# Dense query and output layouts in a fused state-space and attention kernel: both transposed between partitions through DRAM

## The chip, the cores and the metric

The kernel runs on one core of a Trainium2 chip. The metric is the device time of one execution in microseconds (us), and the kernel before is given by the median of three runs. The engines are TensorE (PE; its weight loads are listed as PEld), VectorE (DVE), ScalarE (ACT), GpSimd (POOL) and SyncE (SP), which here issues nearly all DMAs.

## The reference

Two independent parts share a sequence of 2048 rows and a width of 640, and their outputs are put side by side.

```python
# A: complex diagonal state-space layer
h = Lam_bar[None, :] * h + Bu[:, t, :]          # for t in range(2048)
y = 2.0 * einsum("blp,dp->bld", hseq, Cmat).real + x * Dskip
# B: attention, 32 query heads of width 20, one key head and one value head
q = (x @ wq).reshape(B, S, 32, 20).transpose(0, 2, 1, 3)
k = x @ wk ; v = x @ wv                          # [1, 2048, 20]
p = softmax(einsum("bhqd,bkd->bhqk", q, k) * 20 ** -0.5)
o = einsum("bhqk,bkd->bhqd", p, v)
b = o.transpose(0, 2, 1, 3).reshape(B, S, 640) @ wo
```

## The kernel before, in words

**Units.** The queries are cut into 4 blocks of 512 rows (`NQB`), the 32 heads into 8 groups of four (`NGG`), so that there are 32 groups in order. In a group, head j of the four lies on partitions 32j to 32j+31: 20 rows of the head, then one row (row 20), then unused rows. A unit is one head against 128 keys: 4 x 16 = 64 units for each group and 2048 in all. For each unit PE computes 128x512 scores into PSUM, an engine turns them into exponentials in SBUF, and PE multiplies these by the values into the PSUM tile `PV`, whose row 20 of each head collects the softmax denominator.

**Two engines make exponentials.** ACT takes tiles of three and two units (`R`, L1122, `ex_op`) and writes `P`. DVE takes single units (L1127, `dx_op`), which lie in one of the two PSUM banks `B`: it makes a 16-bit integer whose bits are an approximate exponential, and three shifted copies of it (L1132, `sh_op`, up to three units at once, in `Pd`). At most 16 of a group's 64 units may go to DVE (`QUOTA`).

**Who decides.** `main()` is a planner which runs while the program is built. It keeps a modelled clock for each engine, takes the candidate that could begin first (with biases and a little noise drawn from `SEEDS`, one seed for each 64th of the units), and appends it to that engine's list. Each engine then executes its list in order. A unit goes to DVE when DVE's modelled backlog is short and one of the two `B` banks is free. The same two banks serve the query projections, the output projections and all of part A, so each of these holds a bank from its first matmul to its DVE eviction. Threads of background work (`qt`, `norm`, `proj`, and the threads of part A) wait on gates and are mixed in.

**Queries before.** `qt_block` computes one group with `wq4`, the weights padded to 32 columns for each head: five matmuls of 512 columns, one for each 128 of the width; an absolute value on DVE (L702, into `Qabs`); a sixth matmul with `Mblk`, which adds to row 20 a bound of the scores, so that the exponent can't overflow; and a scaling eviction on DVE (L706) into `QT`, a ring of six groups. Group 0 has ACT take the absolute value. The padded weights are copied by DVE (L550) from `wq_raw`, which lies in the tile `OT`.

**Outputs before.** When a group is finished, DVE copies `PV` to `OTr` (L1165). `norm_ops` then sends the four denominator rows to DRAM and reads them back as 128x16, DVE inverts them (L872), and the inverses go to DRAM and come back spread over 32 partitions each (`rwide`, four DMAs). POOL multiplies into `OT` in four pieces of 128 columns (L885). After the eighth group `proj_ops` multiplies `OT` by the padded `WO4`: for each of 4 row tiles and 2 halves of the columns eight matmuls of 320 columns, and a DVE eviction (L936). The last group's denominators are inverted through PE instead (`norm_last`), and `last_ops` does the last block's rest on PSUM that has come free.

**Start and end.** SP issues the transposed loads of x, then `wq`, then ten transposes of part A's input (blocks 0 and 1, `load_xa`), then ten of `BTre` and `BTim`, then `WO4` and ten transposes of C. The first ACT tile starts when keys and the first queries are there.

Of the kernel before, what the change touches and what calls it, by code (L numbers as in the profile page):

```python
# [9 lines left out]
ALU = mybir.AluOpType  # L10
AX = mybir.AxisListType
FP32 = mybir.dt.float32
# [231 lines left out]
class _Kernel:  # L244
# [4 lines left out]
    TILES, PTILES, DUNITS, DSHIFT, QRING = (3, 2), 10, 9, 3, 6  # L249
# [15 lines left out]
    SEEDS = (0, 102003, 103002, 104005, 0, 0, 107005, 0, 109003, 110001, 111003, 112005, 0, 0, 115003, 116004,  # L265
             117001, 118008, 119004, 120009, 121009, 122003, 123005, 124007, 125004, 126001, 127008, 128001,
             129006, 130003, 131008, 132001, 133004, 134007, 135004, 136007, 137001, 138005, 0, 140005, 141001,
             142007, 143003, 144003, 145008, 146005, 147007, 148002, 149003, 150004, 0, 152009, 0, 154009,
             155008, 156002, 157003, 158008, 159005, 160002, 0, 162006, 0, 164007)
# [24 lines left out]
    def alloc(self):  # L294
# [3 lines left out]
                  for i, n in enumerate(self.TILES)]  # L298
# [9 lines left out]
        self.sb("wq4", [128, NC, self.NGG, 128], BF16)  # L308
        self.sb("Mblk", [128, 128], BF16)
        self.sb("mabs", [128, 5], FP32)  # L310
        self.sb("Qabs", [128, 512], I32)

        self.Qpos = self.Qabs[:].bitcast(BF16).rearrange("p (n h) -> p n h", h=2)[:, :, 1]
        self.sb("WO4", [128, self.NGG, 640], BF16)
# [13 lines left out]
        self.sb("OT", [128, self.NGG, 512], BF16)  # L328
        self.wq_raw = self.OT[:].rearrange("p g n -> p (g n)")[:, 0:NC * 640].rearrange("p (c n) -> p c n", c=NC)
        self.part = self.wq4[:].rearrange("p c g n -> p (c g n)").bitcast(FP32)[:, 0:1280].rearrange("p (t n) -> p t n", t=2)  # L330
        self.sb("rden", [128, 2, 16], BF16)
        self.sb("rwide", [128, 512], BF16)
        self.den_rows, self.rec_rows = (nc.dram_tensor(n, (2, 4, 512), BF16, kind="Internal").ap()
                                        for n in ("den_rows", "rec_rows"))
# [29 lines left out]
        self.sb("ystage", [128, 640], BF16)  # L364

# [52 lines left out]
    def setup(self):  # L418
# [44 lines left out]
        dve(lambda e: e.memset(K.wq4[:], 0.0), writes=["wq4"], n=5120, rate=4)  # L463
# [7 lines left out]
        for j in range(4):  # L471
            act(lambda e, j=j: e.activation(K.wk4[:, :, 32 * j:32 * j + 20], K.wk_raw[:, :, :], ACT.Copy),
                ["wk_raw", "wk4"], ["wk4"], n=100)
        ot = [k for g in range(8) for k in self.ot_keys(g)]
        go(self.dma(K.wq_raw, t["wq"].rearrange("(c p) n -> p c n", p=128), "wq", writes=["wq_raw"] + ot, kb=800))
        wq4_0 = K.wq4[:, :, 0, :].rearrange("p c (j r) -> p c j r", r=32)[:, :, :, 0:20]
        self.tables(dve, act, {
            2: lambda: dve(lambda e: e.tensor_copy(wq4_0, K.wq0.rearrange("p c (j r) -> p c j r", r=20)),
                           ["ostage0", "wq4"], ["wq4_0"], n=400, rate=3.5)})
# [44 lines left out]
        for o in copy("act", 0):  # L524
# [14 lines left out]
        wq4_ap = bass.AP(tensor=K.wq4, offset=128, ap=[[NC * self.NGG * 128, 128], [1024, NC], [32, 28], [1, 20]])  # L539
        wqr_ap = bass.AP(tensor=K.OT, offset=80, ap=[[self.NGG * 512, 128], [640, NC], [20, 28], [1, 20]])  # L540
# [9 lines left out]
            Op("dve", lambda e: e.tensor_copy(wq4_ap, wqr_ap), ["wq_raw", "wq4"] + ot, ["wq4_4"], occ=dve_t(2800, 3.5))])  # L550
# [5 lines left out]
        for b in range(2):  # L556
            for o in self.load_xa(b):
                go(o)
        for c in range(NC):
            go(self.dma(K.BTre[:, c, :], t["bre"][:, 128 * c:128 * (c + 1)], f"bre{c}", writes=[f"BTre{c}"],  # L560
                        tr=True, kb=160))
            go(self.dma(K.BTim[:, c, :], t["bim"][:, 128 * c:128 * (c + 1)], f"bim{c}", writes=[f"BTim{c}"],
                        tr=True, kb=160))

# [123 lines left out]
    def qt_block(self, qb, gg, hold=None, gate=None, done=None):  # L688
# [7 lines left out]
        def mm(c):  # L696
            return self.mms([self.m1(lambda: h.T[:, :], K.wq4[:, c, gg, :], K.xbT[:, c, 512 * qb:512 * qb + 512],
                                     c == 0, False)], ["wq4_0" if gg == 0 else "wq4_4"] + xs, [None], accum=c > 0,
                            lock=c == 0, gate=gate if c == 0 else None, hold=h)
# [3 lines left out]
                                                      op0=ALU.bitwise_and), [None], ["Qpos"], occ=dve_t(512), hold=h),  # L703
# [4 lines left out]
        ]  # L708


    def scan_ops(self):
# [5 lines left out]
        self.prog = prog = dict(x=1, a=0, u=0, s=0, r=0, y=0, w=0, c=0)  # L717
# [13 lines left out]
        for gg in range(self.NGG):  # L731
            pool(lambda e, gg=gg: e.memset(K.WO4[:, gg, :], 0.0), [], ["WO4"] + old, 240)
        wov = t["wo"].rearrange("(gg jr) n -> jr gg n", jr=80)
        for j in range(4):
            sc_.append(self.dma(K.WO4[32 * j:32 * j + 20, :, :], wov[20 * j:20 * j + 20, :, :], f"wo{j}", reads=["WO4"],
                                writes=[f"WO4_{j}"], kb=200))
# [32 lines left out]
        sx = [o for b in (2, 3) for o in self.load_xa(b, lambda b=b: prog["y"] >= 4 * (b - 1), lambda b=b: prog.update(x=b))]  # L769
# [87 lines left out]
    def ot_keys(self, gg):  # L857

        return [f"OT{gg}{h}" for h in self.PIECES]

    def norm_ops(self, g):

        K, sl, gg = self, g % 2, g % self.NGG
        if g == self.NQB * self.NGG - 1:
            return self.norm_last(g)
        den, rec = self.den_rows[sl], self.rec_rows[sl]
        rows = bass.AP(tensor=K.OTr, offset=2 * 512 * self.DH + 512 * sl, ap=[[32 * 2 * 512, 4], [1, 512]])
        flat = lambda x: x.rearrange("j (b n) -> (j b) n", n=16)

        def recip(e):  # L870
            with self.nc.allow_low_precision("bf16 reciprocal of softmax denominator"):
                return e.reciprocal(K.rden[:, sl, :], K.rden[:, sl, :])  # L872
        ops = [self.dma(den, rows, f"den{sl}", reads=[f"OTr{sl}"], writes=[f"den{sl}"], kb=4),
               self.dma(K.rden[:, sl, :], flat(den), f"dens{sl}", reads=[f"den{sl}"], writes=[f"rden{sl}"], kb=4),
               Op("dve", recip, [f"rden{sl}"], [f"rden{sl}"], occ=0.17),
               self.dma(flat(rec), K.rden[:, sl, :], f"rec{sl}", reads=[f"rden{sl}"], writes=[f"rec{sl}"], kb=4)]
        for j in range(4):
            wide = bass.AP(tensor=rec.tensor, offset=rec.offset + 512 * j, ap=[[0, 32], [1, 512]])
            ops.append(self.dma(K.rwide[32 * j:32 * j + 32, :], wide, "rwide", reads=[f"rec{sl}"], writes=[f"rwide{j}"],
                                kb=32))  # L880
        n = 512 // len(self.PIECES)
        gate = lambda: g < self.NGG or g // self.NGG - 1 in self.projected
        for i, h in enumerate(self.PIECES):
            c = slice(n * i, n * i + n)
            ops.append(Op("pool", lambda e, c=c: e.tensor_tensor(K.OT[:, gg, c], K.OTr[:, sl, c], K.rwide[:, c], ALU.mult),  # L885
                          [f"OTr{sl}", *(f"rwide{j}" for j in range(4))], [f"OT{gg}{h}"], occ=max(0.2, n / 450.0 + 0.1),
                          gate=None if i else gate))
        ops[-1].done = lambda: self.normed.add(g)
        return ops

    def norm_last(self, g):
        K = self
        sl, rs, gg = g % 2, g % 2, g % self.NGG
# [8 lines left out]
        def wide(t, j):  # L902
# [5 lines left out]
        ops.append(Op("dve", lambda e: e.tensor_tensor(K.OT[:, gg, :], K.OTr[:, sl, :], h1.T[:, :], ALU.mult),  # L908
                      [None, f"OTr{sl}"], self.ot_keys(gg), occ=dve_t(512), free=True, hold=h1,
# [3 lines left out]
    def proj_ops(self, qb, ggs, part=False):  # L913

        K = self
        ops = []
        wo = ["WO4"] + [f"WO4_{j}" for j in range(4)]
        ots = [k for gg in ggs for k in self.ot_keys(gg)]
        for ts in ((2, 3) if part else range(4)):
            st = ts % 2  # L920
            t0 = 512 * qb + 128 * ts
            for h in range(2):
                hd = Hold()
                lst = [self.m1(lambda hd=hd: hd.T[:, 0:320], K.OT[:, gg, 128 * ts:128 * ts + 128],
                               K.WO4[:, gg, 320 * h:320 * h + 320], gg == ggs[0], gg == ggs[-1]) for gg in ggs]
                have = lambda: all(self.NGG * qb + gg in self.normed for gg in ggs) and (
                    not part or len(self.qt_done) == self.NQB * self.NGG)
# [6 lines left out]
                if part:  # L934
                    dst, keys = K.part[:, st, 320 * h:320 * h + 320], [f"part{st}", "wq4_0", "wq4_4"]
# [7 lines left out]
    def last_ops(self, gates, normed):  # L943

        K = self
        wo = ["WO4"] + [f"WO4_{j}" for j in range(4)]
# [4 lines left out]
        def mm(ts, gg, begin):  # L951
            return self.mms([self.m1(banks[ts][h], K.OT[:, gg, 128 * ts:128 * ts + 128],
                                     K.WO4[:, gg, 320 * h:320 * h + 320], begin, gg == self.NGG - 1) for h in range(2)],
                            self.ot_keys(gg) + wo, keys[ts], accum=not begin, gate=lambda: gates[ts]() and normed(gg))

        threads = []
        for ts in (3, 0, 2, 1):
            t0 = 512 * (self.NQB - 1) + 128 * ts
            first = 0 if ts < 2 else self.NGG - 2
# [426 lines left out]
```

## Time and profile before

| what | value |
|---|---|
| median of 3 runs | 780.4 us (780.14 to 781.43) |
| profiled execution, own time | 780.05 us |
| its span, first to last instruction | 778.3 us |
| granted TensorE clock, mean | 0.993 |
| busy: PE, DVE, ACT, POOL | 698.2, 711.2, 763.1, 450.9 us |
| first ACT tile starts, last one ends | 21.95 us, 768.56 us |
| units through ACT, through DVE | 1647, 401 |
| moved by DMA | 21.08 MB, mean 27 GB/s |

The span is what the profile covers; the own time of the execution is 1.75 us longer. "Busy" is the time in which an engine executes at least one instruction. In the groups of instructions, the columns are line, engine, operation, output and input with their shapes, count, then busy time and mean duration of one in ns, and last the idle time of the engine just before them with what ended it. Durations of neighbours on one engine can overlap by some tens of ns. The unit counts are those of the PV matmuls that read `P` (1647), and of L1127 (401).

### The profile page before, as it was taken

The numbers are of one execution on the slowest core, as the hardware profiler recorded it, in microseconds if no ns is written. First come the engines' busy times: TensorE is split into PE (matmuls) and PEld (weight loads), VectorE is DVE, ScalarE is ACT, GpSimd is POOL, SyncE is SP. The second block draws the span as 40 slices with busy tenths as digits, with TensorE's granted clock in tenths as the row PEclk, the third lists the DMA queues.
The fourth block names the chain that finished last, engine by engine and source line by source line (L and its number), as shares of the span: only waits on it lengthen the run. The fifth ranks groups of instructions, "written<-read, shape, count | busy, mean of one in ns | idle before, by whom it ended". The sixth has DMA issues, their size and how long they took to land.

```text
span 778.3 us, 16683 instructions
## 1 busy us (share of the span) xinstructions
PE 698.2 (90%) x6474; PEld 219.3 (28%) x6538; DVE 711.2 (91%) x1270; ACT 763.1 (98%) x692; POOL 450.9 (58%) x897
## 2 busy tenths in 40 slices
PE   5898887888889999988889999998899999899887
PEld 1322222222223332322223323222233332233223
DVE  7789999999999888899999888999998899998995
ACT  7999999999999999999999999999999999999995
POOL 4418836998995030398895005999960799910010
PEclk9799999999999999999999999999999999999999
DMA  9781000000000000110000001100000000000001
GB/s 191 120 137 27 8 2 8 15 3 9 8 9 18 18 25 17 46 22 9 1 9 17 25 19 39 40 5 9 9 17 25 11 26 10 24 17 25 11 12 38
DMA packets 57877, 21.08 MB, mean 27 GB/s; under 512 B 48332, under 2 KB 57800, under 8 KB 57800
## 3 DMA queue, kind: packets, MB, share of 16 engines
q1 hardware_dynamic: 55658, 19.70, 11.8%
q8 instruction: 52, 0.85, 0.5%
q10 hardware_dynamic: 2142, 0.32, 0.3%
q14 instruction: 25, 0.20, 0.1%
HBM read 5.99 MB, written 5.50 MB: 15 GB/s over the span
## 4 chain that ended last, share of the span: by engine, by line
ACT 86%; DVE 6%; PE 5%; SPq 1%; DMA 1%; issue 1%; DVEq 0%
ACT P L1122 86%; PE R L409 2%; DVE Pd L1132 2%; DVE Pd L1127 2%; PE PV L409 1%; SPq L390 1%; PE B L409 1%; DVE tm L790 1%; DMA xbT<-in_B_x_dram 1%; DVE hh L817 0%; DVE mabs L518 0%; DVE CGre L749 0%; DVE ostage L936 0%; DVE QT L706 0%; DVE CGim L749 0%
## 5 line engine op out<-in xcount | busy, mean ns | idle before, releaser
L1122 ACT ACTIVATE P<-R 128x1536 bf16<-128x1536 f32 (+1 forms) x659 | 745.5, 1443 | 1.5 <-PE B L409 0.7
L409 PE MATMUL R<-QT,KT 32*128 32x512 bf16 (+1 forms) x1647 | 258.6, 387 | 55.5 <-ACT P L1122 45.7
L1127 DVE TENSOR_SCALAR Pd<-B 128x512 int16<-128x512 f32 x401 | 272.1, 683 | 36.4 <-PE B L409 32.1
L1132 DVE TENSOR_SCALAR Pd<-Pd 128x1536 int16<-128x1536 int16 (+2 forms) x534 | 256.9, 514 | 1.0
L409 PE MATMUL PV<-P,VP 128*32 128x512 bf16 x1647 | 246.2, 387 | 1.2 <-issue 0.5
L409 PE MATMUL PV<-Pd,VP 128*32 128x512 bf16 x1604 | 244.9, 384 | 2.4 <-DVE OTr L1165 1.4
L806 POOL TENSOR_TENSOR tm<-hh,cs 128x128 bf16<-128x128 f32 x320 | 161.5, 525 | 12.8 <-DVE hh L817 3.3
L409 PE MATMUL B<-QT,KT 32*128 32x512 bf16 x401 | 154.2, 384 | 0.0
L409 PEld LDWEIGHTS R<-QT,KT 32*128 32x128 bf16 (+1 forms) x1647 | 63.5, 91 | 294.6 <-ACT P L1122 285.6
L885 POOL TENSOR_TENSOR OT<-OTr,rwide 128x128 bf16<-128x128 bf16 x124 | 60.4, 506 | 137.7 <-DMA rwide<-rec_rows 72.5
L806 POOL TENSOR_TENSOR uh<-tm 128x128 bf16<-128x128 bf16 x160 | 80.3, 520 | 72.1 <-DVE tm L790 67.6
L806 POOL TENSOR_TENSOR W<-tm 128x128 bf16<-128x128 bf16 x160 | 90.8, 589 | 13.8 <-PE B L409 9.5
L409 PEld LDWEIGHTS PV<-Pd,VP 128*32 128x32 bf16 x1604 | 58.4, 94 | 62.5 <-issue 39.3
L409 PEld LDWEIGHTS PV<-P,VP 128*32 128x32 bf16 x1647 | 57.7, 94 | 60.5 <-issue 46.7
L747 POOL TENSOR_SCALAR tm<-W,sc 128x128 f32<-128x128 bf16 x40 | 30.8, 783 | 37.0 <-DMA W<-in_A_C_im_dram 19.4
L790 DVE TENSOR_TENSOR tm<-B,cs 128x1024 bf16<-128x1024 f32 x40 | 48.5, 1213 | 2.2 <-PE B L409 2.1
L409 PE MATMUL B<-CGre,W 128*128 128x384 bf16 (+1 forms) x160 | 46.4, 305 | 0.0
L409 PE MATMUL B<-CGim,W 128*128 128x384 bf16 (+1 forms) x160 | 45.5, 299 | 0.0
L409 PE MATMUL B<-xbT,wq 128*128 128x512 bf16 x141 | 41.9, 384 | 3.4 <-issue 1.9
L409 PE MATMUL B<-WO,OT 128*128 128x320 bf16 x220 | 41.0, 302 | 0.0
L817 DVE TENSOR_TENSOR_SCAN hh<-sc,hini,uh 128x512 f32<-128x512 f32 x30 | 40.9, 1365 | 0.0
L409 PEld LDWEIGHTS B<-QT,KT 32*128 32x128 bf16 x401 | 36.3, 90 | 0.0
(130 smaller groups left out, 411.8 us busy)
## 6 DMA issues: line engine op xcount, KB each, us to landing
rwide<-rec_rows SPq DMA_DIRECT2D x124, 32.0 KB, 1.9
out_dram<-ystage SPq DMA_DIRECT2D x16, 160.0 KB, 1.8
out_dram<-ostage SPq DMA_DIRECT2D x12, 160.0 KB, 1.8
OT<-in_B_wq_dram SPq DMA_DIRECT2D x1, 800.0 KB, 6.3
WO<-in_B_wo_dram SPq DMA_DIRECT2D x4, 200.0 KB
den_rows<-OTr SPq DMA_DIRECT2D x31, 4.0 KB
rden<-den_rows SPq DMA_DIRECT2D x31, 4.0 KB, 1.7
rec_rows<-rden SPq DMA_DIRECT2D x31, 4.0 KB, 1.4
```

Of the source, the lines that this page charges most:

```text
L390: return e.dma_start_transpose(out_ap, in_ap)
L409: ins = e.matmul(o() if callable(o) else o, lhsT=l, rhs=r, start=st, stop=sp, skip_group_check=True, **kw)
L747: pool(lambda e, y=y, c=c, gy=gy, i=i: e.tensor_scalar(K.ctmp[:, i:i + 128], y[:, i:i + 128], sc[:, gy, c:c + 1], None, op0=ALU.mult), key ...
L790: dve(lambda e, k=k, h=h: e.tensor_tensor(K.tm[:, 2 * k:2 * k + 2, :], bass.AP(tensor=K.BB, offset=512 * int(h.key[1]), ap=[[512 * self.BA ...
L806: put(lambda e, c0=c0, end=end: e.tensor_tensor(out[:, c0:end], a[:, c0:end], b[:, c0:end], op), reads, [writes + h], n, gate=None if i el ...
L817: dve(lambda e, ri=ri, ini=ini: e.tensor_tensor_scan(K.hh[:, ri, :], dec, K.uh[:, ri, :], ini, ALU.mult, ALU.add), ["sc", *(f"uh{ri}{h}" f ...
L885: ops.append(Op("pool", lambda e, c=c: e.tensor_tensor(K.OT[:, gg, c], K.OTr[:, sl, c], K.rwide[:, c], ALU.mult), [f"OTr{sl}", *(f"rwide{j ...
L1122: return Op("act", lambda e: e.activation(dst, K.R[n % 2][:, 0:512 * size], ACT.Exp, scale=self.exp_scale), [f"R{n % 2}"] + ["R0c"] * (siz ...
L1127: return Op("dve", lambda e: e.tensor_scalar(K.Pd[:, 0, u, :], K.B[x][:, :], self.d_off, 0.0, op0=ALU.add, op1=ALU.max), [f"B{x}"], [f"Pd{ ...
L1132: return Op("dve", lambda e: e.tensor_scalar(K.Pd[:, i, a:b, :], K.Pd[:, 0, a:b, :], float(self.SHIFTS[i]), 0.0, op0=ALU.subtract, op1=ALU ...
```

## The change

The queries of a block are computed without padding and brought to the padded layout by a trip through DRAM; the outputs go through DRAM in the other direction and are projected in a dense layout.

- **Queries.** Groups 0 and 1 keep the old path (weights `wq0p` and `wq1`). For the rest `qd_block` computes a whole block: `wqd` holds the weights with heads innermost, made by five copies on POOL, and five dense tiles of 128 rows take five matmuls and one DVE eviction each into `Qd`. The bound for all 32 heads takes five 16-bit absolute values on DVE and five matmuls with `Md`, and one DVE eviction (`Gs`). Four DMAs write `Qd` and one writes `Gs` to DRAM (`Qs`), and `qr_ops` reads one group at a time into `QT`, now a ring of four. The next block's rows are written when all groups of the block before have been read.
- **Outputs.** A group's `OTr` goes to DRAM whole (`Os`). After the eighth group `dense_ops` reads the denominators (`rwide`, four DMAs) and the outputs (`OTd`, four DMAs) of the block densely, DVE inverts 128x512 at once, and POOL multiplies 5 x 4 pieces. `proj_ops` then takes five matmuls where it took eight. In the last block the groups 6 and 7 take the path of `norm_last` into `OTp`; five dense parts and two padded ones make the sum.
- **Setup.** `wq_raw` lies in the ACT tiles `P7` to `P9` instead of `OT`; new memsets, masks and small DMAs make `Md` and the constant rows in DRAM (`dense_setup`). Part A's input of block 1 is loaded by the planner's thread `sx` and no longer ahead of `BTre`. `WO4` takes eight DMAs instead of four.
- **Planner.** The thread `qt` joins those that can keep units from DVE when they wait for a bank (`starved`); SP's issues for these trips go first; `SEEDS` are others.

```diff
-    TILES, PTILES, DUNITS, DSHIFT, QRING = (3, 2), 10, 9, 3, 6
+    TILES, PTILES, DUNITS, DSHIFT, QRING = (3, 2), 10, 9, 3, 4
...
-        self.wq_raw = self.OT[:]...
+        self.wq_raw = self.P[:].rearrange("p s n -> p (s n)")[:, 18 * 512:18 * 512 + NC * 640].rearrange("p (c n) -> p c n", c=NC)
...
-            Op("dve", lambda e: e.tensor_copy(wq4_ap, wqr_ap), ["wq_raw", "wq4"] + ot, ["wq4_4"], occ=dve_t(2800, 3.5))])
+            Op("dve", lambda e: e.tensor_copy(pad(K.wq1[:]), K.wq_raw[:, :, 80:160].rearrange("p c (j r) -> p c j r", r=20)),
+               ["wq_raw", "wq1"] + pk, ["wq1"], occ=dve_t(400, 3.5))])
+        for c in range(NC):
+            pool(lambda e, c=c: e.tensor_copy(K.wqd[:, c, :].rearrange("p (d h) -> p d h", h=32),
+                                              K.wq_raw[:, c, :].rearrange("p (h d) -> p d h", d=20)),
+                 ["wq_raw"] + pk, [f"wqd{c}"], occ=1.6)
+        self.dense_setup(pool)
-        for b in range(2):
-            for o in self.load_xa(b):
-                go(o)
+        for o in self.load_xa(0):
+            go(o)
...
+    def qd_block(self, qb):
+        gate = lambda: self.units >= 64 * (self.NGG * (qb - 1) + 1)
+        for m in range(NC):
+            h = Hold()
+            for c in range(NC):
+                ops.append(self.mms([self.m1(lambda h=h: h.T[:, :], K.wqd[:, c, 128 * m:128 * m + 128],
+                                             K.xbT[:, c, 512 * qb:512 * qb + 512], c == 0, c == NC - 1)],
...
+            ops.append(Op("dve", lambda e, m=m, h=h: e.tensor_scalar(K.Qd[:, m, :], h.T[:, :], self.c1, None, op0=ALU.mult),
+                          [None], [f"Qd{m}"], occ=dve_t(512), free=True, hold=h))
+        read = lambda: self.qread >= self.NGG * qb
...
+        seq = ["a", "a", "g", "a", "g", "a", "g", "a", "g", "g"]
...
+    def qr_ops(self, g, done):
+        return [self.dma(K.QT[:, r, :], K.Qs[0, 128 * (g % self.NGG):128 * (g % self.NGG) + 128, :], f"QT{r}",
...
+                         gate=lambda: g // self.NGG in self.qsent and self.units >= 64 * (g - self.QRING + 2))]
...
     def norm_ops(self, g):
-        ops = [self.dma(den, rows, ...), self.dma(K.rden[:, sl, :], flat(den), ...),
-               Op("dve", recip, [f"rden{sl}"], [f"rden{sl}"], occ=0.17),
-               self.dma(flat(rec), K.rden[:, sl, :], ...)]
+        return [self.dma(self.Os[qb, 128 * gg:128 * gg + 128, :], self.OTr[:, g % 2, :], f"Os{g % 2}", reads=[f"OTr{g % 2}"],
+                         writes=[f"Os{qb}_{gg}"], kb=128, done=lambda: self.normed.add(g))]
+    def dense_ops(self, qb):
+        for dd in range(4):
+            ops.append(self.dma(K.rwide[32 * dd:32 * dd + 32, :], src, "rwide", ...))
+        for dd in range(4):
+            ops.append(self.dma(K.OTd[32 * dd:32 * dd + 32, :, :], src, "OTd", ...))
+                return e.reciprocal(K.rwide[:], K.rwide[:])
+        ops.append(Op("dve", recip, rw, rw, occ=dve_t(512)))
+        for i, h in enumerate(self.PIECES):
+            for m in range(NC):
+                ops.append(Op("pool", lambda e, c=c, m=m: e.tensor_tensor(K.OTd[:, m, c], K.OTd[:, m, c], K.rwide[:, c], ALU.mult),
...
-                lst = [self.m1(..., K.OT[:, gg, 128 * ts:128 * ts + 128], K.WO4[:, gg, 320 * h:320 * h + 320], ...) for gg in ggs]
+                lst = [self.m1(lambda hd=hd: hd.T[:, 0:320], K.OTd[:, m, 128 * ts:128 * ts + 128],
+                               K.WO4[:, m, 320 * h:320 * h + 320], m == 0, m == NC - 1) for m in range(NC)]
...
         self.starved = dict(sy=r.choice((0.0, 1.0, 4.0, 99.0)), sa=r.choice((2.0, 99.0)),
-                            proj=r.choice((0.0, 1.0, 4.0, 99.0)))
+                            proj=r.choice((0.0, 1.0, 4.0, 99.0)),
+                            qt=r.choice((0.0, 1.0, 4.0, 99.0)))
...
+                if o.eng == "sp" and name in ("qt", "qr", "norm", "dense"):
+                    bias = -2.0
+                elif name == "qt" and not self.qsent:
+                    bias -= 0.1
```

`dve_t(n, rate)` is the planner's price of a DVE instruction, n / (960 x rate) + 0.07 us.

## The prediction

> **What bounds the kernel now.** I read the page from the top: busy shares, slices, chain of waits, then the groups of instructions.
>
> ```profile
> span 778.3 us, 16683 instructions
> PE 698.2 (90%) x6474; PEld 219.3 (28%) x6538; DVE 711.2 (91%) x1270; ACT 763.1 (98%) x692; POOL 450.9 (58%) x897
> DVE  7789999999999888899999888999998899998995
> ACT  7999999999999999999999999999999999999995
> ...
> ACT 86%; DVE 6%; PE 5%; SPq 1%; DMA 1%; issue 1%; DVEq 0%
> ...
> L1122 ACT ACTIVATE P<-R 128x1536 bf16<-128x1536 f32 (+1 forms) x659 | 745.5, 1443 | 1.5 <-PE B L409 0.7
> L1127 DVE TENSOR_SCALAR Pd<-B 128x512 int16<-128x512 f32 x401 | 272.1, 683 | 36.4 <-PE B L409 32.1
> L1132 DVE TENSOR_SCALAR Pd<-Pd 128x1536 int16<-128x1536 int16 (+2 forms) x534 | 256.9, 514 | 1.0
> ```
>
> ACT makes exponentials from 21.95 to 768.56 us, 746.6 us, and in these it idles for about 1. So the span is 22 us of start, the ACT tiles, and 9.7 us of tail, and the middle is shortened only by giving units to DVE. One unit costs ACT 745.5/1647 = 0.453 us, and DVE (272.1 + 256.9)/401 = 1.32 us. DVE is full early and has room later, as the view by stages (PE, PEld, DVE, ACT, POOL) shows:
>
> ```profile
> 120.00:160.00 40.00, 32.91 (x331) 8.97 (x332) 39.44 (x69) 39.78 (x36) 35.10 (x62) 1.00 0.05 11
> 440.00:480.00 40.00, 39.03 (x354) 12.93 (x350) 33.92 (x70) 40.00 (x37) 7.13 (x16) 1.00 0.07 22
> ```
>
> From 60 to 760 us DVE idles 47 us in all, most of it where PE is full (at 440) and nearly always waiting for PE's scores (L1127 above, 32.1 us).
>
> The rate of exchange: x us of DVE freed become units; a unit also shortens the loop by 0.453 us, of which DVE would have used 93%. So x us give 0.453 x/(1.32 + 0.42) = 0.26 x. The sum is made against the profiled execution's 780.05 us (span plus 1.75), 0.35 below the median of 780.4.
>
> **DVE's work.**
>
> ```profile
> L706 DVE TENSOR_SCALAR QT<-B 128x512 bf16<-128x512 f32 x32 | 21.8, 682 | 2.8 <-PE B L409 2.6
> L702 DVE TENSOR_SCALAR Qabs<-B 128x512 int32<-128x512 int32 x31 | 21.0, 679 | 1.2 <-PE B L409 1.2
> L872 DVE RECIPROCAL rden<-rden 128x16 bf16<-128x16 bf16 x31 | 7.5, 241 | 0.0
> L1132 DVE TENSOR_SCALAR Pd<-Pd 128x512 int16<-128x512 int16 x141 | 44.3, 354 | 0.2
> L550 DVE COPY wq<-OT 128x2800 bf16<-128x2800 bf16 x1 | 1.3, 1319 | 0.0
> ```
>
> Removed: 30 evictions of L706 (20.5), 30 of L702 (20.4), 31 small inversions (7.5), the copy L550 (1.3): 49.7 us. Added: 20 dense evictions and 4 of Gs at 0.682 (16.4), 20 absolute values at the row of the same shape and type, 0.354 (7.1), one more norm_last, 0.26 + 0.69 (L900, L908), and the copy of wq1, 0.35: 24.8. The four 512-wide inversions stand in the planner at dve_t(512) = 0.60 each, 2.4. It deals out units by what it believes: 49.7 - 24.8 - 2.4 = 22.5 us free, times 0.26 = **-5.9**.
>
> **What the inversion really takes.** No row has it. From below it is a pass of 512 (0.68 as L706). From above it is 32 of the 16-wide ones by their spacing, 5.1. In the timeline both sizes are seen with the next instruction right behind:
>
> ```profile
> 22.65 0.18 DVE L667 RECIPROCAL sc<-sc 128x5 f32<-128x5 f32 x1
> 22.75 1.37 DVE L509 TENSOR_SCALAR KT<-B,half 128x512 bf16<-128x512 f32 x2
> ...
> 84.68 0.24 DVE L872 RECIPROCAL rden<-rden 128x16 bf16<-128x16 bf16 x1
> 84.84 0.50 DVE L1132 TENSOR_SCALAR Pd<-Pd 128x1536 int16<-128x1536 int16 x1
> ```
>
> Spacing 0.10 for 5 elements and 0.16 for 16: 5.5 ns for an element, where L1127's spacing of 0.60 is 1.2. So I take 0.07 + 512 x 0.0055 = 2.9. That is 2.3 us later than planned, four times, and behind it in DVE's list stand the evictions of score banks; PE executes in order, so its next ACT tile waits too. ACT has about one tile in hand (1.23 to 1.65 us long, PE refilling for 0.4), some 0.9. Some slips fall on DVE's own idle time, so I take 0.75 of ACT idle each, **+3.0**, bounds 0 and 4 x 2.3 = 9.2. The Trainium skill (VectorE: DVE Perf Modes, First, the fixed hardware budget) says the inversion divides iteratively with a repeat count of 8, while simple operations take one slice. Read as 8 cycles at the page's 0.96 GHz it would be an estimated 4.3 us and the slip 3.7; the spacing of 0.16 allows less than 8 cycles.
>
> **PE and its banks.** 192 matmuls for queries and bounds (the 32 with Mblk among them) become 132, 60 fewer at 0.384; the output projection has 80 fewer at 0.302 (8 to 5 in three and a half blocks). By durations 47 us, less by spacing since they overlap; ACT hides them. But DVE waits for PE, so part of its 47 us of idle time becomes units. In the timeline of 34 to 52 us a query group holds a bank for 4.3 us, and one D unit at a time gets through; a dense tile should take half (no absolute value, no sixth matmul), though the bound matmuls hold one for some 8 us in each block. Bounds: nothing, and all 47 x 0.26 = 12. I take 6 us recovered, **-1.6**, nearer to nothing, because parts of A fill the same banks.
>
> **Tail.** 40 output matmuls at the end become 36, at 5.5/34 = 0.16 each: **-0.6**. Group 6's norm_last lies inside the loop, and the dense path of the last block needs some 18 us (two DMA trips, inversion, 20 POOL pieces at 0.49) after group 29, with two groups of 23 us to cover it.
>
> **Costed at nothing.** POOL: 124 pieces become 80, 21 us less, off the path. Its five wqd copies wait for wq (issued 14.1, 6.3 to landing) and must end before the eighth ACT tile overwrites P7, at 21.95 + 3.5 x 2.26 = 29.9. Nearest rows: the cast of 512 (L447, 0.61), 0.76 each, done by 25; and five L747 pieces of 0.65, 3.3 each, done by 37, a stall of 7. I take the cast: one source, one pass. SP: 217 issues go (31 of each small trip, 124 rwide), 125 come (20 of Qs, 30 of QT, 30 of Os, 32 dense, 9 at setup, 4 more for WO4). The issue of Ms waits for mabs (19.8) and md for Ms's landing; behind them stand part A's input and the ten BTre/BTim transposes. These started at 14.75 and ended at 42.6; with five inputs moved behind they end at about 24 + 15 x 1.3 = 44. Only part A waits, and in that stage DVE isn't full (17.6 of 20 us); without that cover it is 1.5 us of DVE, 0.4 of time. The five moved inputs cost SP 1.4 each later, hidden by the same. Stores of OTr and reads of QT wait behind each other on SP, with a group (23 us) to spare against DMA landings of 1.9.
>
> Sum: 780.05 - 5.9 + 3.0 - 1.6 - 0.6 = **775.0**.
>
> **Rivals.**
> - *Banks were the real limit.* If half or more of DVE's idle time turns into units, -6 or more stands for -1.6: 770, and down to 764 at all of it. For it: 32.1 us of waits for PE. Against: those stages carry part A's output matmuls. Chance 0.18.
> - *Group 2's queries come late.* (Slower.) Before, group 2's scores begin at about 72 us (OTr of group 1 at 75.2). Now its queries need wqd, five dense tiles at 2.3 to 4 us from about 37 (done 48 to 57), the bound chain of ten steps (5 to 11 us), store and read at 2 us each beside transposes: 57 to 72. If it lands after 72, ACT idles for every us of it, and every later block has a whole block as margin, so it is paid once. DVE units held back while `qt` waits add to it, 0.45 each. Ten us late, by slower tiles or DMAs, gives 785; it loses against no change from 5 us on. For it: DMA share 0.87 from 40 to 60. Against: the planner prices all of these. Chance 0.18.
> - *The inversion blocks more.* By the upper row, 5.1 each, the slip is 4.5, less 0.9 in hand: 4 x 3.6 = 14.4, so 780.05 - 8.1 + 14.4 = 786; it turns the sign from 2 us of stall each. By the page's 8 cycles, 4 x 2.8 = 11 gives 783. The two spacings speak against it. Chance 0.09.
> - *The gain isn't dealt out*: the planner's other seeds or the quota of 16 leave the D units at about 401, and only tail and stalls remain: 780 to 782. Chance 0.10.
>
> The forecast, 771 to 779, has 0.45. A difference below 0.2% (1.6 us) can't be told from no change here. Faster: 0.45 + 0.18 = 0.63; same 0.10; slower 0.27. The range leaves out the far ends of the first and of the slower rivals: 766 to 785.
>
> **What would show it.** L1127's count at 401 + 14 to 20 and L1122's units down by as many. L706 and L702 at two rows or fewer, dense evictions x20, reciprocal 128x512 at about 2.9 with ACT idle behind it. First exponentials of group 2 without a gap at 70 to 75. DVE idle from 60 to 760 below 47. The forecast is wrong if L1122 idles over 5 us in the loop or the D count doesn't rise.

## The result, and the profile after

The changed kernel takes 785.95 us (median of 4 runs, 785.37 to 786.59), where four runs of the kernel before have a median of 780.57: a ratio of 1.0068, 95% interval [1.005, 1.0085]. It is slower by 5.4 us; 775.0 was forecast. Its profiled execution took 786.13 us, with a span of 784.4 and a mean granted clock of 0.989.

First the page of the changed kernel, in the order in which the page of before was read: span, busy shares, slices, chain of waits, groups. L1232 is now ACT's exponential, L1237 and L1242 are DVE's; L418 is the helper that records every matmul.

```profile
span 784.4 us, 16444 instructions
PE 686.8 (88%) x6429; PEld 214.1 (27%) x6500; DVE 707.0 (90%) x1206; ACT 760.4 (97%) x688; POOL 440.8 (56%) x865
DVE  6599899999988988899997978899999889998896
ACT  7999999999989999999998999999999999999995
...
ACT 68%; DVE 16%; PE 8%; POOL 2%; DMA 2%; SPq 2%; issue 1%; POOLq 0%; DVEq 0%
...
L1232 ACT ACTIVATE P<-R 128x1536 bf16<-128x1536 f32 (+1 forms) x655 | 742.4, 1418 | 11.3 <-PE B L418 9.3
L1237 DVE TENSOR_SCALAR Pd<-B 128x512 int16<-128x512 f32 x412 | 278.4, 682 | 32.2 <-PE B L418 28.4
L1242 DVE TENSOR_SCALAR Pd<-Pd 128x1536 int16<-128x1536 int16 (+2 forms) x501 | 256.8, 546 | 1.2
```

Every engine's busy time is lower than before (for PE this says little, as both traces lack some matmul records), and yet the span is 6.1 us longer. The reader is to look at L1232's last column: ACT idles 11.3 us just before these instructions, where it was 1.5. The chain of waits says the same: the chain ran through ACT for 86% of the span and now for 68%, and DVE's share went from 6 to 16. DVE took 412 units instead of 401, ACT 1636 instead of 1647. The sum by ACT's loop: busy -3.1, idle +9.8, tail -0.5 (9.26 after 9.74), start -0.1, together +6.1.

The groups kept apart by shape show the change's own instructions:

```profile
L765 DVE TENSOR_SCALAR Qd<-B 128x512 bf16<-128x512 f32 x20 | 13.7, 687 | 3.4 <-PE B L418 3.1
L982 DVE RECIPROCAL rwide<-rwide 128x512 bf16<-128x512 bf16 x4 | 13.4, 3342 | 0.0
L778 DVE TENSOR_SCALAR Qabs<-Qd 128x512 int16<-128x512 int16 x20 | 6.8, 341 | 0.5
L562 POOL COPY wqd<-P 128x640 bf16<-128x640 bf16 x5 | 6.5, 1329 | 9.6 <-DMA P<-in_B_wq_dram 9.5
L787 DVE CAST Gs<-B 32x512 bf16<-32x512 f32 x4 | 2.7, 672 | 0.5 <-PE B L418 0.5
```

An inversion takes 3.34 us. The timeline of DVE around the first one, and then that of ACT in the same stretch (start, time, instruction; in brackets the idle time before it and what ended it):

```profile
223.16 0.98 DVE L1242 TENSOR_SCALAR Pd<-Pd 128x1024 int16<-128x1024 int16 x2
224.06 3.34 DVE L982 RECIPROCAL rwide<-rwide 128x512 bf16<-128x512 bf16 x1
227.33 1.76 DVE L1242 TENSOR_SCALAR Pd<-Pd 128x1024 int16<-128x1024 int16 x3
229.22 1.41 DVE L1237 TENSOR_SCALAR Pd<-B 128x512 int16<-128x512 f32 x2
```

```profile
213.55 13.93 ACT L1232 ACTIVATE P<-R 128x1536 bf16<-128x1536 f32 x12
229.22 2.37 ACT L1232 ACTIVATE P<-R 128x1536 bf16<-128x1536 f32 x2 [1.74 <-PE B L418]
232.01 8.23 ACT L1232 ACTIVATE P<-R 128x1536 bf16<-128x1536 f32 x7 [0.42 <-PE B L418]
```

PE's waits between 225 and 234 us, and between 413 and 423 (us in total, times, longest), name what connects the two:

```profile
PE PV L418 <- DVE Pd L1242: 2.4, 1, 2.4
```

```profile
PE R L418 <- DVE ystage L949: 2.0, 1, 2.0
```

The shifted copies (L1242) of a unit stood behind the inversion. A PV matmul needed them, PE waited 2.4 us with ACT's next scores queued behind that matmul, and ACT ran dry. At the other three inversions PE's next scores waited for an eviction of part A (L949) instead, 2.0, 1.7 and 1.7 us. So the instruction that is held up differs, and the effect is the same. ACT behind the other three:

```profile
418.03 1.02 ACT L1232 ACTIVATE P<-R 128x1024 bf16<-128x1024 f32 x1 [1.35 <-PE B L418]
420.53 13.76 ACT L1232 ACTIVATE P<-R 128x1536 bf16<-128x1536 f32 x12 [1.47 <-PE B L418]
...
606.65 1.02 ACT L1232 ACTIVATE P<-R 128x1024 bf16<-128x1024 f32 x1 [0.87 <-PE B L418]
608.07 12.75 ACT L1232 ACTIVATE P<-R 128x1536 bf16<-128x1536 f32 x11 [0.40 <-PE B L418]
...
749.69 25.45 ACT L1232 ACTIVATE P<-R 128x1536 bf16<-128x1536 f32 x23 [1.20 <-PE B L418]
```

The four inversions (at 224.06, 413.62, 601.85 and 745.35 us) have 1.2 to 2.8 us of ACT gaps behind them, 7.5 us in all. Each inversion ends 2.74 us later than planned, 11.0 us in all, so some 0.9 us of each was covered. Another 2.1 us lie between 34 and 45 us; the first run below has the same lists and 0.75 there, so I don't lay them to the lists.

DVE's freed time became fewer units than forecast. The windows from 60 to 760 us (PE, PEld, DVE, ACT, POOL), of the kernel before and then of the changed one, show DVE idle for 47.4 and 53.5 us:

```profile
60.00:760.00 700.00, 637.98 (x5968) 198.09 (x6029) 652.56 (x1145) 698.99 (x619) 427.47 (x837) 1.00 0.06 16
60.00:760.00 700.00, 622.06 (x5864) 191.47 (x5929) 646.50 (x1078) 691.41 (x611) 416.65 (x803) 1.00 0.12 32
```

### The profile page after: what moved, and what is told of

Same layout as the page of the kernel before. It is cut to its first block, busy times and chain, and to the rows that moved or that the text cites. A ratio compares the mean times of both kernels' runs of the same rounds, so it can differ in the third digit from the quotient of the medians.

```text
span 784.4 us, 16444 instructions
## 1 busy us (share of the span) xinstructions
PE 686.8 (88%) x6429; PEld 214.1 (27%) x6500; DVE 707.0 (90%) x1206; ACT 760.4 (97%) x688; POOL 440.8 (56%) x865
## 2 busy tenths in 40 slices
DMA packets 59610, 31.23 MB, mean 40 GB/s; under 512 B 39942, under 2 KB 59534, under 8 KB 59534
## 3 DMA queue, kind: packets, MB, share of 16 engines
q1 hardware_dynamic: 57392, 29.86, 15.7%
## 4 chain that ended last, share of the span: by engine, by line
ACT 68%; DVE 16%; PE 8%; POOL 2%; DMA 2%; SPq 2%; issue 1%; POOLq 0%; DVEq 0%
ACT P L1232 68%; DVE Pd L1237 5%; DVE Pd L1242 4%; PE R L418 3%; PE B L418 3%; PE PV L418 2%; DVE rwide L982 2%; DVE hh L915 1%; POOL tm L845 1%; SPq L399 1%; DMA md<-m_row 1%; DVE tm L888 1%; DMA xbT<-in_B_x_dram 1%; POOL uh L904 1%; DMA o_rows<-OTr 0%
## 5 line engine op out<-in xcount | busy, mean ns | idle before, releaser
L1232 ACT ACTIVATE P<-R 128x1536 bf16<-128x1536 f32 (+1 forms) x655 | 742.4, 1418 | 11.3 <-PE B L418 9.3
L418 PE MATMUL R<-QT,KT 32*128 32x512 bf16 (+1 forms) x1636 | 258.1, 388 | 68.3 <-ACT P L1232 47.9
L1237 DVE TENSOR_SCALAR Pd<-B 128x512 int16<-128x512 f32 x412 | 278.4, 682 | 32.2 <-PE B L418 28.4
L1242 DVE TENSOR_SCALAR Pd<-Pd 128x1536 int16<-128x1536 int16 (+2 forms) x501 | 256.8, 546 | 1.2
L418 PE MATMUL PV<-Pd,VP 128*32 128x512 bf16 x1648 | 251.1, 385 | 2.6 <-DVE OTr L1275 1.2
L418 PE MATMUL PV<-P,VP 128*32 128x512 bf16 x1636 | 248.8, 387 | 3.2 <-DVE Pd L1242 2.7
L904 POOL TENSOR_TENSOR tm<-hh,cs 128x128 bf16<-128x128 f32 x320 | 165.6, 540 | 22.9 <-DVE hh L915 10.1
L418 PE MATMUL B<-QT,KT 32*128 32x512 bf16 x412 | 159.5, 387 | 0.0
L418 PEld LDWEIGHTS R<-QT,KT 32*128 32x128 bf16 (+1 forms) x1636 | 64.2, 91 | 305.9 <-ACT P L1232 274.5
L904 POOL TENSOR_TENSOR uh<-tm 128x128 bf16<-128x128 bf16 x160 | 82.1, 534 | 81.8 <-DVE tm L888 77.4
L418 PEld LDWEIGHTS PV<-Pd,VP 128*32 128x32 bf16 x1648 | 59.5, 94 | 66.4 <-issue 40.9
L418 PEld LDWEIGHTS PV<-P,VP 128*32 128x32 bf16 x1636 | 57.5, 94 | 60.2 <-issue 42.3
L989 POOL TENSOR_TENSOR OTd<-OTd,rwide 128x128 bf16<-128x128 bf16 x80 | 32.7, 436 | 51.4 <-DVE rwide L982 49.5
L418 PE MATMUL B<-CGre,W 128*128 128x384 bf16 (+1 forms) x160 | 46.5, 305 | 0.1
L418 PE MATMUL B<-CGim,W 128*128 128x384 bf16 (+1 forms) x160 | 45.6, 299 | 0.0
L915 DVE TENSOR_TENSOR_SCAN hh<-sc,hini,uh 128x512 f32<-128x512 f32 x30 | 40.4, 1345 | 0.0
L418 PEld LDWEIGHTS B<-QT,KT 32*128 32x128 bf16 x412 | 37.3, 91 | 0.0
L418 PE MATMUL B<-xaT,BTre 128*128 128x512 bf16 x89 | 27.2, 383 | 2.1 <-issue 1.3
L418 PE MATMUL B<-xaT,BTim 128*128 128x512 bf16 x85 | 27.1, 392 | 2.2 <-issue 1.7
```

Of the source, the lines that this page charges most:

```text
L418: ins = e.matmul(o() if callable(o) else o, lhsT=l, rhs=r, start=st, stop=sp, skip_group_check=True, **kw)
L904: put(lambda e, c0=c0, end=end: e.tensor_tensor(out[:, c0:end], a[:, c0:end], b[:, c0:end], op), reads, [writes + h], n, gate=None if i el ...
L915: dve(lambda e, ri=ri, ini=ini: e.tensor_tensor_scan(K.hh[:, ri, :], dec, K.uh[:, ri, :], ini, ALU.mult, ALU.add), ["sc", *(f"uh{ri}{h}" f ...
L989: ops.append(Op("pool", lambda e, c=c, m=m: e.tensor_tensor(K.OTd[:, m, c], K.OTd[:, m, c], K.rwide[:, c], ALU.mult), rw + [f"OTe{dd}" for ...
L1232: return Op("act", lambda e: e.activation(dst, K.R[n % 2][:, 0:512 * size], ACT.Exp, scale=self.exp_scale), [f"R{n % 2}"] + ["R0c"] * (siz ...
L1237: return Op("dve", lambda e: e.tensor_scalar(K.Pd[:, 0, u, :], K.B[x][:, :], self.d_off, 0.0, op0=ALU.add, op1=ALU.max), [f"B{x}"], [f"Pd{ ...
```

## The experiments

Eleven runs; each ratio is to the kernel before on the same chip.

**e1: the inversion replaced by a copy, the lists left as they are** (so the dense groups stay unnormalised).

```diff
-                return e.reciprocal(K.rwide[:], K.rwide[:])
+                return e.tensor_copy(K.rwide[:], K.rwide[:])
```

> The changed kernel with every list of instructions as it is, but the four 512-wide inversions are copies of the same tile (under 0.6 us instead of 3.34). The dense groups' outputs are therefore multiplied by their denominators. Theory A (the inversion takes 3.34 us where the planner reckons 0.60, and the score evictions behind it stop PE and then ACT): ACT's idle time of 7.5 us right behind the four inversions goes, 785.95 - 7.5 = 778.5, 777 to 780. Rival B (the idle time belongs to the block boundary itself: DRAM trips, banks, the dense projection): under 2 us change, 784 or more.

776.8 us, ratio 0.9957 [0.9942, 0.9972]. Its groups and ACT's timeline in the stretch shown above:

```profile
L982 DVE COPY rwide<-rwide 128x512 bf16<-128x512 bf16 x4 | 1.6, 400 | 0.0
...
L1232 ACT ACTIVATE P<-R 128x1536 bf16<-128x1536 f32 (+1 forms) x655 | 741.5, 1435 | 2.5 <-PE B L418 0.9
```

```profile
216.64 24.36 ACT L1232 ACTIVATE P<-R 128x1536 bf16<-128x1536 f32 x21
```

21 tiles without a gap. Taking 4 x 2.94 = 11.8 us off DVE took 9.2 us off the time, with all else in its order (8.7 when each is held against the kernel before as measured with it). This alone is more than the loss of 5.4. Of the 9.2, the gaps behind the inversions are 7.5, and the smaller gaps between 34 and 45 us are 1.4. The time is 0.2 us below the range expected.

**e2 and e3: the same length added elsewhere.** An unread maximum over 3100 elements (3.37 us), which the planner doesn't know of, ahead of each inversion: in the changed kernel (e2), and in the kernel before at groups 7, 15, 23 and 29 (e3).

```diff
+                e.tensor_reduce(out=K.scr[:, qb:qb + 1], in_=K.cs[:].rearrange("p c r n -> p (c r n)")[:, 0:3100],
+                                axis=AX.X, op=ALU.max)
```

> The changed kernel with all lists as they are, and ahead of each of the four inversions a reduction over 3100 elements that nobody reads (about 3.3 us of DVE, which the planner doesn't know of). A: the slack is used up already, so ACT waits for nearly all of it: 785.95 + 4 x 3.2 = 798.8, 796 to 800. B: the inversion wasn't on the path, so part of the added time is still absorbed: under 792.

> The kernel before with all lists as they are, and at groups 7, 15, 23 and 29 the same unread reduction of some 3.3 us ahead of the small inversion. A: layout is not needed for the loss, an unplanned hold of DVE at the same four places is enough: the part that is late beyond 0.9 us in hand, 4 x 2 to 4 x 3 us, 788.5 to 792.5. B: the old layout absorbs it in DVE's idle time: under 784.

e2: 804.14 us, ratio 1.0305 [1.029, 1.032]. e3: 793.86 us, ratio 1.0175 [1.0158, 1.0192]. So 13.5 us more on DVE cost 18.2 us in the changed kernel (its profiled clock was 0.97, which may be part of it) and 13.8 in the kernel before. Both times lie above their expected ranges. e3's exponential row and ACT's timeline at the first place:

```profile
L1126 ACT ACTIVATE P<-R 128x1536 bf16<-128x1536 f32 (+1 forms) x659 | 746.9, 1416 | 12.6 <-PE B L410 11.4
```

```profile
219.57 4.94 ACT L1126 ACTIVATE P<-R 128x1536 bf16<-128x1536 f32 x4
226.52 14.09 ACT L1126 ACTIVATE P<-R 128x1536 bf16<-128x1536 f32 x12 [2.01 <-PE B L410]
```

The kernel before shows the same picture without any dense layout: its ACT gaps behind the four places are 10.4 us for 13.5 us held. By the times, unplanned DVE time costs 0.8 to 1.35 us per us. By ACT's gaps alone, the changed kernel and e3 cover 0.8 to 0.9 us of each hold on the average, the size of the tile in hand, and nothing more is absorbed. In e2, where two such pieces stand in a row, even that cover is gone: 25.1 us of gaps for 24.4 us late.

**e7 and e11: the wide inversion kept, but planned.** The planner is told 3.27 us and its `SEEDS` are searched again, in the model alone; two lists of that search were run.

```diff
-        ops.append(Op("dve", recip, rw, rw, occ=dve_t(512)))
+        ops.append(Op("dve", recip, rw, rw, occ=3.27))
```

> The changed kernel, all instructions as they are and the wide inversion kept, but the planner is told 3.27 us for it instead of 0.60, and its tie-breaking numbers are searched again in the same way; planner's end 765.6 us. Theory (it was not the 3.3 us themselves that cost 9 us but that the lists did not know of them): ACT idle behind the four inversions under 3 us in all, D units 407 to 411, 776 to 780 us. Rival (3.3 us of DVE at one stretch stop PE through the score banks however they are planned): 1 us or more of ACT idle behind each inversion, 782 or above.

> The changed kernel with the wide inversion known to the planner at 3.27 us, under another searched list (planner's end 765.85 us). By the end plus 14.6: 778.5 to 782.5. Theory (a planned inversion stops nobody): again under 3 us of ACT idle in all within 8 us behind the four inversions. Rival (the lack of idle was luck of one list): 4 us or more there, 783 or above.

780.72 us, ratio 1.0002 [0.9993, 1.0012], and 777.97 us, 0.9973 [0.9961, 0.9984]. The first is 0.7 us above its range. DVE's timeline at the first inversion of e7, then ACT's:

```profile
222.40 0.69 DVE L1233 TENSOR_SCALAR Pd<-B 128x512 int16<-128x512 f32 x1
223.00 3.35 DVE L978 RECIPROCAL rwide<-rwide 128x512 bf16<-128x512 bf16 x1
226.26 1.22 DVE L1233 TENSOR_SCALAR Pd<-B 128x512 int16<-128x512 f32 x2
```

```profile
218.76 24.35 ACT L1228 ACTIVATE P<-R 128x1536 bf16<-128x1536 f32 x21
```

The instruction is as long as ever, and ACT makes 21 tiles without a gap: before it DVE has finished what PV needs, and behind it stand only fresh scores. In other places of the two lists an eviction of part A or a shifted copy does stand right behind the inversion, but PE waits for no DVE instruction there for more than 0.3 us. In both lists ACT has no gap within 8 us behind any of the eight inversions, while all twelve unplanned holds (the changed kernel, e2, e3) have one. The rival, that 3.3 us at a stretch stop PE however they are planned, falls. What costs is that the order was made for 0.60. The price and the new search came together, and no newly searched list was run with 0.60; that a new order alone would do is made unlikely by the count, not excluded. Two expectations were missed: e7 has 415 units where 407 to 411 were named, and e11's time lies 0.5 us below its range.

**e4 and e8: the inversion made 128 wide.** The denominators are read as 128x128 (`rn`), inverted, written back (`Rs`) and from there read wide into `rwide`.

```diff
+        for q in range(4):
+            ops.append(self.dma(K.rn[32 * q:32 * q + 32, :], src, "rn", ...))
+        ops.append(Op("dve", recip, rn, rn, occ=0.87))
+        for q in range(4):
+            ops.append(self.dma(dst, K.rn[32 * q:32 * q + 32, :], "Rs", ...))
```

> The changed kernel with the 512-wide inversion taken off DVE: the denominators of a block are read from DRAM as 128 partitions by 128, inverted there (planned at 0.87 us), written back and read wide, by four DMAs each way; the computation is complete. The planner's tie-breaking numbers were searched again, so the lists differ from those of the changed kernel; the planner's own end is 761.3 us where it has 764.1 for the changed kernel and 769.4 for the kernel before. In the kernel before the time is 11 us above that end, and with the copy in place of the inversion 12.7. Theory (the unplanned length of the inversions is what made the change slower): inversions of about 0.8 us, L1232-row idle under 3 us in the loop, D units at or above 412, 772 to 776 us. Rival (the wide DVE pass is not the point, the dense outputs' chain itself, DMAs and POOL pieces, makes PE and ACT late at the same places): idle of 5 us or more behind the inversions remains and the time is 780 or above.

> The complete kernel with the 128-wide inversion once more, under the second list of the same search (planner's end 764.7 us). The four searched lists run so far took 13.6 to 15.2 us above the planner's end. Theory (the time of a searched list is the planner's end plus 14.6, within 2): 777 to 781.5, D units 415 to 423, and no ACT idle of over 1 us right behind an inversion. Rival (the 776.0 was one lucky list and the form itself is worth no more than the kernel with the wide inversion planned): 782 or above.

**e5 and e9: the outputs' part alone**, with this inversion; queries by `qt_block` with `wq4`, as in the kernel before. `wq_raw` in the ACT tiles and the planner's priority for SP's issues stay as in the changed kernel. **e6 and e10: the kernel before**, nothing but its `SEEDS` searched again. Against the changed kernel, and against the kernel before:

```diff
-        self.sb("wqd", [128, NC, 640], BF16)
-        self.sb("wq1", [128, NC, 128], BF16)
+        self.sb("wq4", [128, NC, self.NGG, 128], BF16)
...
-    def qd_block(self, qb):
...
+    def qt_block(self, qb, gg, hold=None, gate=None, done=None):
```

```diff
-    SEEDS = (0, 102003, 103002, 104005, 0, 0, 107005, ...)
+    SEEDS = (552717, 524792, 197878, 942524, 286453, 991798, ...)
```

> The outputs' part alone: outputs dense through DRAM, projection over five parts, the 128-wide inversion of the run before; queries stay as in the kernel before (32 evictions and 31 absolute values of 512, five to six query matmuls a group), with six steps of the P ring for queries instead of four. Lists searched in the same way, planner's end 764.2 us. If the query part is what frees DVE (theory: 21 of the 22.5 us freed are its evictions and absolute values), the D units fall back to about 401 to 404 and the time is 777 to 780. Rival (the outputs' part carries the gain, through DVE's small inversions and PE's shorter projection): D units 410 or more and 775 to 777 us, as the planner has it, within 2 us of the run before.

> The outputs' part alone under another searched list (planner's end 765.2 us). By the end plus 14.6: 778 to 782. Theory (the outputs' part alone gives DVE about 10 units more than the kernel before): D units 408 to 415. Rival (the 413 of the other list came from its order): D units 400 to 405 and over 782.

> The kernel before with nothing but its planner's tie-breaking numbers searched again, in the way used for the two runs before; planner's end 770.3 us against 769.4 with its own numbers. It tells what the search alone is worth. Theory (a new order is worth what the planner says, plus or minus 2 us): 779.5 to 783. Rival (lists searched here hold up differently on the chip than the shown ones): outside of this, and then the two runs before must be read against this one and not against the kernel before.

> The kernel before under another searched list (planner's end 771.2 us). By the end plus 14.6: 784 to 788, D units 399 to 405. Rival (searched lists of the kernel before are as good as its own, and the 783.9 was a bad one): 780 to 782.

| kernel, two searched lists each | us | ratios with 95% intervals | units on DVE |
|---|---|---|---|
| before (e6, e10) | 783.93, 784.33 | 1.0061 [1.0036, 1.0087], 1.0057 [1.0033, 1.0081] | 403, 403 |
| outputs alone (e5, e9) | 779.43, 777.39 | 0.9984 [0.9975, 0.9993], 0.9967 [0.9955, 0.9979] | 413, 409 |
| all, 128-wide inversion (e4, e8) | 776.0, 779.46 | 0.9943 [0.9928, 0.9957], 0.9986 [0.9977, 0.9996] | 421, 413 |
| all, wide inversion planned (e7, e11) | 780.72, 777.97 | 1.0002 [0.9993, 1.0012], 0.9973 [0.9961, 0.9984] | 415, 410 |

e4 beats both kernels. Its rows:

```profile
L1239 ACT ACTIVATE P<-R 128x1536 bf16<-128x1536 f32 (+1 forms) x651 | 737.8, 1397 | 4.4 <-PE B L416 3.3
L1244 DVE TENSOR_SCALAR Pd<-B 128x512 int16<-128x512 f32 x421 | 283.9, 682 | 31.2 <-PE B L416 27.4
...
L977 DVE RECIPROCAL rn<-rn 128x128 bf16<-128x128 bf16 x4 | 3.8, 942 | 0.0
```

Its idle time of 4.4 us is above the 3 expected, in no gap of over 1 us; e8's is 2.9. e8's time came as expected, its 413 units are two short of the range.

Three things follow. Two lists of one kernel lie up to 3.5 us apart, so one list proves a part only if it gives more. (Their profiled clocks lie between 0.982 and 0.993, which may be part of the spread.) Searched in one way, the changed kernel with the 128-wide inversion is 6.4 us faster than the kernel before (means 777.7 and 784.1), with the wide inversion planned 4.8 us, and the outputs' part alone has 5.7. With two lists for each these sizes are rough, but all six changed lists lie below both lists of the kernel before. And the kernel before is 3.6 us better under its own seeds than under these: e6 lies above its expected range, and the rival "as good" of e10 falls. The planner's own ends account for 1.4 us of that (769.4 against 770.3 and 771.2). Why its own lists hold up better on the chip beyond this (ACT idle 1.5 us against 6.5 and 6.7) was not found.

For e5 I had expected the units to fall back to 401 to 404, since it keeps the long query work on DVE. They did not; the rival's 410 or more came, though not its 775 to 777 us: the time lies in the range of the theory. e9's units came as expected, its time 0.6 us below the range. The scores row of DVE in e6 and in e5, whole span:

```profile
L1123 DVE TENSOR_SCALAR Pd<-B 128x512 int16<-128x512 f32 x403 | 274.3, 684 | 39.1 <-PE B L405 34.6
```

```profile
L1164 DVE TENSOR_SCALAR Pd<-B 128x512 int16<-128x512 f32 x413 | 280.1, 683 | 36.0 <-PE B L407 33.2
```

From 60 to 750 us the windows give DVE 48.9 and 49.7 us of idle time in the kernel before (e6, e10), 40.4 and 43.3 with the outputs alone, and 44.9 and 46.9 with both parts. So with the outputs alone DVE idles 6 to 9 us less. Over the whole span DVE is as busy as before with 8 units more (712.9 and 713.0 us in e6 and e10, 715.7 and 710.2 in e5 and e9). Units are only some half of the gain: by their rows, ACT's exponentials are 3.3 us less busy than in e6 and e10 on the average, and idle 2.9 us less just before them. How much of the shorter waits is due to the layout and how much to the order of the lists is not shown.

## Why the prediction was wrong

- **Failed step: what the inversion really takes, +3.0.** The length was near, 3.34 us against 2.9, so that each inversion is 2.74 us late where 2.3 was forecast. "ACT has about one tile in hand ... some 0.9" fits: 7.5 us of idle for 11.0 us late leave some 0.9 each. What failed is "some slips fall on DVE's own idle time", which halved the rest to 0.75: all four left gaps, 1.9 us of ACT idle each on the average. So the term is +7.5, of which the missing discount makes about 2.6 and the length 1.8. The 9.2 of e1 equals the forecast's upper bound by chance: it holds 1.4 us of other gaps.
- **Second failed step: the units, -5.9 and -1.6.** 13 units from DVE's freed work and 3.5 from PE's relief were forecast; 11 came, and ACT's busy time fell by 3.1 us instead of 7.5. Of PE's relief nothing shows in this kernel: DVE's idle time from 60 to 760 us was to fall by 6 us from 47.4, and rose to 53.5. In e1, without the long inversion, it is 57.3, while DVE is busy 15.7 us less than before. So part of the freed time was not dealt out as units, which is part of what the rival "the gain isn't dealt out" says.
- **Where it turned the sign.** With 7.5 in place of 3.0 the sum would be 779.5, hardly a gain; 4.4 us fewer from the units make it a loss, and 2.3 us of other ACT gaps, mostly between 34 and 45 us, were not in the sum. e1 shows the rest without the inversion: 3.3 us faster than before, where the sum has 8.1 without its +3.0.
- **Rate of exchange and size of the gain.** Under equally searched lists the change is worth 6.4 us and 14 units with a short inversion. So -8.1 was sized some 2 us too large; most of the rest of the gap to e1's 3.3 is that the shown kernel before has lists better than those searched here, by 3.6 us.
- **How the gain splits: wrong.** Nearly all of -5.9 was to come from queries. The outputs alone give 5.7 us and 8 units, the queries another 0.7 us and 6 units, less than two lists differ. The saving at the banks was put at 6 us of DVE idle time; the outputs' part alone recovers 6 to 9, both parts together 2 to 5. With the queries on top DVE is busy 8.6 us less (704.4 us on the average after 713.0), so much of the query work freed (some 17 us by the forecast's rows) stays idle time. Why the planner and the chip make so few units of it stays open.
- **Tail -0.6**: measured -0.5.
- **Costed at nothing.** The five POOL copies took 1.33 us each, not 0.76, and ended at 26.4, ahead of 29.9: no stall. Part A's transposes ended at 48.8 us instead of 44; DVE made 39 units from 20 to 110 us where it had made 42, but the kernel before makes 39 there too under other lists (e6, e10), so this isn't shown to have a price.
- **Rivals.** "The inversion blocks more" named 786, and 786.0 came, by luck: its inversion of 5.1 us was to cost 14.4 us against a gain of 8.1; measured are 3.34 us, 7.5 us of gaps and a gain of less than half. "Group 2's queries come late" is refuted: they landed at about 65 us, and ACT has no gap from 45 to 80. "Banks were the real limit" fits the direction of the outputs' part, not its size, and the cause there is not isolated.
- **The Trainium skill** (VectorE: DVE Perf Modes, First, the fixed hardware budget) has a repeat count of 8 for the division. Here 128 elements take 942 ns and 512 take 3342: 6.25 ns for each further element, so the reading as 8 cycles (4.3 us) is too long and the forecast's 5.5 ns too short. The spacing of 0.16 us for 16 elements did not by itself decide between them: it does so only with the 0.07 us that the forecast took as fixed.

## What to carry to other kernels

When an order of instructions is made by a planner, look up each new instruction's price in it against the longest time that the trace allows: a us which the planner doesn't know of costs about a us on the bound engine, even on another engine that idles elsewhere, and the same us costs little once the order is made for it. Count the bound engine's tile in hand as cover once (here some 0.9 us), but not the late engine's idle time elsewhere, when that engine feeds a queue that executes in order. And judge a layout change under lists searched alike for both sides: here the seeds are worth 3.6 us, more than half of the change.

## What the runs showed of the hardware that I had not expected

- The inversion's time grows by 6.25 ns an element (241 ns for 16, 942 for 128, 3342 for 512), while a copy of the same 128x512 takes 400 ns: 8 times less.
- A 128x640 copy on POOL which swaps the order of heads and columns took 1.33 us, 1.7 times what a cast row led me to expect.
- The added DMA traffic (31.23 MB instead of 21.08) hardly shows: DMA has 2% of the chain of waits after 1%, the dense reads of 160 KB landed 3.4 us after issue, the group reads of 128 KB after 2.2.
